# State-space scan into a bilinear feed-forward: the two pairs of a 128-token block share one group of state products and run feed-forward over 512 tokens from block 2 on

## The chip, the cores and the metric

The kernel runs on one core of a Trainium2 chip. Times are device microseconds of one execution; lower is better. Three timed executions of the kernel before are shown, and one profiled execution.

## The reference, cut to what matters

Inputs are x (4 batches, 8 heads, 768 positions, 32 values), a decay a per position, and B and C (16 state values per position). For each batch and head a state of 16 x 32 is carried along the sequence; within a chunk each position also sees the earlier positions through C·B weighted by the decay between them. The result y, put together over the heads to rows of 256, goes through a bilinear feed-forward:

```
cum = cumsum(log a) in the chunk;  L = exp(cum_i - cum_j), i >= j
y   = ((C B^T) * L) x  +  (C state) * exp(cum)
state = exp(sum log a) * state + sum_j exp(cum_last - cum_j) B_j x_j
x2  = y, all heads of a token side by side        (3072 tokens, 256)
out = ((x2 @ w_a) * (x2 @ w_b)) @ w_out           (256 -> 1536 -> 256)
```

The chunk length does not change the mathematics; the kernel uses 128 positions.

## The kernel before, in words

**Tiling.** The sequence is cut into six blocks of 128 positions, and the four batches into two pairs, so there are twelve pairs p = 0 to 11; pair p belongs to block p // 2. A pair is 256 tokens: two batches, 128 positions. Inside a pair the positions are held as 64 partitions times two (r), batch after batch, so that 128 partitions hold both batches. All matrix operands are in 16-bit floats, all sums in 32-bit PSUM.

**Steps of one pair.** `load` (L131) brings B, C and x in six transfers from SP's queue. GpSimd scales B and C by the decay factors and x by a constant (`scale_bc`, `scale_x`, L238 to L269), writing B and C as six 128-column planes; `turn` (L306) transposes the planes with one DMA transpose, also from SP. `scores` (L312) makes C·B for all eight heads in 32 small matmuls into four PSUM banks (SC0 and SC1, two banks each; bank m holds heads 2m and 2m+1). `mask` (L345) multiplies a bank by the causal mask and puts it into SBUF as 16-bit (tile T1): VectorE does it, or, with by_pool, ScalarE copies the bank to SBUF and GpSimd multiplies. `outputs` (L418) then writes y into the first 128 columns of the same four banks: 8 matmuls of the carried state with C (L425), 32 of T1 with x (`pv_u`, L363), and 16 for the new state sums (`ds_mm`, L380) into columns 256 to 319 of two of the banks. ScalarE moves y to SBUF (tile X2T, three instructions, L441); VectorE adds the new state sums to the carried state (`state_sums`, L468, tile U), and GpSimd prepares from it the state operand of the next block (`state_spread`, L484, and the decayed copy gU, L491).

**Feed-forward.** A unit (L529) is two of the twelve 128-wide slices of d_ff for the 256 tokens of a pair: four matmuls of 256 columns with w_a into a PSUM bank, four with w_b into another (L504), a ScalarE copy of the first to SBUF (L518, tile asb), and a VectorE product of the second with it (L525, tile hk). Six units make a pair. `out_half` (L557) multiplies the hidden values of 128 tokens with w_out in twelve matmuls of 256 columns (L538), ScalarE scales the result to SBUF (L553) and SP's queue stores it.

**PSUM.** Four of the eight banks are SC0 and SC1. The other four are a pool (psf) which every unit takes two of and every out_half one, in turn; so a bank is written again four takings later, and only once ScalarE or VectorE has read it.

**Order.** The kernel is scheduled by hand: each engine runs its instructions in the order in which the program issues them. The start (pairs 0 to 2, weights, factors) is written out. From pair 3 on one loop (L704) does, for each pair p: scores of p; GpSimd's preparation and the transpose of p+1, the state operand of p-1, the loads of p+2; then the masks of p between the units of pair p-1 and the first output half of p-2; outputs and state sums of p; the second output half of p-2; the last two units of p-1. The last pair's feed-forward stands after the loop.

The SBUF pool `mid` (three buffers per tile name) holds T1, the scaled x and B, the transposed planes and GpSimd's temporary; `ffh` (four buffers) holds hk, asb and the output rows.

Of the kernel before, what the change touches and what calls it, by code (L numbers as in the profile page):

```python
# [22 lines left out]
def kernel(  # L23
# [60 lines left out]
    X2T = big.tile([128, NP, 2, 2, Q], f16, name="X2T")  # L84
# [17 lines left out]
    mid = ctx.enter_context(tc.tile_pool(name="mid", bufs=3))  # L102
    ffh = ctx.enter_context(tc.tile_pool(name="ffh", bufs=4))
    ps4 = ctx.enter_context(tc.tile_pool(name="ps4", bufs=1, space=PSUM))
# [313 lines left out]
    def outputs(p):  # L418
        s = st[p]
        SCt = (SC0, SC1)  # L420
        for m in range(4):
            for bt in range(2):
                rows = slice(32 * m, 32 * m + 32)
                half = 64 * ((m + bt) % 2)
                nc.tensor.matmul(  # L425
                    SCt[bt][half : half + 64, m // 2, 0:Q],
                    s["Sbd"][rows, bt],
                    s["CT"][rows, bt],
                    start=True,
                    stop=False,  # L430
                    skip_group_check=True,
                    tile_position=(32 * m, half),
                )
        py = {(bt, u): SCt[bt][:, u, 0:Q] for bt in range(2) for u in range(2)}
        for u in range(2):
            pv_u(p, u, py, False)
        if p // NBP < NBLK - 1:
            ds_mm(p, 256, [SC0[:, 1], SC1[:, 1]])
        whole, low, high = slice(0, 128), slice(0, 64), slice(64, 128)
        for bt, to, fr in ((0, whole, whole), (1, low, high), (1, high, low)):  # L440
            nc.scalar.activation(  # L441
                out=X2T[to, p, bt].rearrange("p u (i r) -> p u r i", r=2),
                in_=SCt[bt][fr, :, 0:Q].rearrange("p u (r i) -> p u r i", r=2),
                func=AF.Copy,
                scale=YS / XS,
            )
# [114 lines left out]


# [141 lines left out]
    for p in range(3, NP):  # L704
        scores(p)
        ri = p >= P0
        if p + 1 < NP:
            scale_bc(p + 1, 1, nc.gpsimd)
            scale_bc(p + 1, 0, nc.gpsimd)
            turn(p + 1)  # L710
        if (p - 1) // NBP < NBLK - 1:
            state_spread(p - 1)
        if p + 1 < NP:
            scale_x(p + 1, nc.gpsimd)
        if p + 2 < NP:
            load(p + 2)
        if p == 3:
            mask(product(p, 0))
            h()
            for m in range(1, 4):  # L720
                mask(product(p, m))
            out_half(1, 0)
            out_half(1, 1)
            go((2, 2))
        else:
            h = unit(p - 1, 0)
            mask(product(p, 0), ri=ri)
            h()
            mask(product(p, 1), ri=ri)
            mask(product(p, 2), ri=ri)  # L730
            h = unit(p - 1, 1)
            h()
            mask(product(p, 3), ri=ri)
            go((p - 1, 2))
            out_half(p - 2, 0)
            go((p - 1, 3))
        pull(p)
        outputs(p) if ri else pv(p)
        if p // NBP < NBLK - 1:
            state_sums(p)  # L740
        if p == 3:
            go((2, 3))
        else:
            out_half(p - 2, 1)
        if p % 2 == 0 and p // 2 + 1 < NBLK:
            fb(p // 2 + 1)
        go((p - 1, 4), (p - 1, 5))

    go((NP - 1, 0), (NP - 1, 1))
    out_half(NP - 2, 0)  # L750
    go((NP - 1, 2), (NP - 1, 3))
    out_half(NP - 2, 1)
# [51 lines left out]
```

## Time and profile before

| | |
|---|---|
| three timed executions | 127.15, 129.27, 129.0 us; median 129.0 |
| profiled execution, its own time | 127.25 us |
| its span in the profile | 125.5 us |
| TensorE (PE) busy | 119.9 us, 96% |
| weight loads (PEld) busy | 101.3 us, 81% |
| VectorE (DVE) busy | 88.8 us, 71% |
| ScalarE (ACT) busy | 72.5 us, 58% |
| GpSimd (POOL) busy | 56.6 us, 45% |
| granted TensorE clock in the profiled execution | 1.0 |

Times of the profile count from the start of the span. Matmuls are pipelined: the start of one to the start of the next is what one costs, and the duration printed for one (273 ns for 256 columns) is longer than that. A timeline line merges instructions of one kind that follow each other: start, length, engine, line, shapes, count, and in brackets how long the engine had been idle and what ended it. "SPq" is SP's queue issuing a DMA.

### The profile page before, as it was taken

The numbers are of one execution on the slowest core, as the hardware profiler recorded it, in microseconds if no ns is written. First come the engines' busy times: TensorE is split into PE (matmuls) and PEld (weight loads), VectorE is DVE, ScalarE is ACT, GpSimd is POOL, SyncE is SP. The second block draws the span as 40 slices with busy tenths as digits, with TensorE's granted clock in tenths as the row PEclk, the third lists the DMA queues.
The fourth block names the chain that finished last, engine by engine and source line by source line (L and its number), as shares of the span: only waits on it lengthen the run. The fifth ranks groups of instructions, "written<-read, shape, count | busy, mean of one in ns | idle before, by whom it ended". The sixth has DMA issues, their size and how long they took to land.

```text
span 125.5 us, 4786 instructions
## 1 busy us (share of the span) xinstructions
PE 119.9 (96%) x1964; PEld 101.3 (81%) x1964; DVE 88.8 (71%) x165; ACT 72.5 (58%) x144; POOL 56.6 (45%) x100
## 2 busy tenths in 40 slices
PE   6979999999999999999999999999999999999990
PEld 2436789978898988888898898889889889899980
DVE  1588978894958958948959949959849739644440
ACT  0466666866365575575575475485485575674430
POOL 7999974957850933806508307508218000000000
PEclk9999999999999999999999999999999999999999
DMA  3999999974644666547646764454646210110112
GB/s 65 167 167 232 157 213 159 184 145 80 167 89 67 165 115 125 141 71 185 81 74 169 87 107 128 88 108 126 114 82 168 66 42 5 42 42 5 44 45 78
DMA packets 45493, 13.79 MB, mean 110 GB/s; under 512 B 40496, under 2 KB 45264, under 8 KB 45472
## 3 DMA queue, kind: packets, MB, share of 16 engines
q1 hardware_dynamic: 41520, 10.06, 38.4%
q0 software_dynamic: 1952, 3.08, 14.6%
q10 hardware_dynamic: 2000, 0.36, 1.6%
q8 instruction: 15, 0.25, 0.9%
q14 instruction: 6, 0.05, 0.1%
HBM read 11.13 MB, written 3.15 MB: 114 GB/s over the span
## 4 chain that ended last, share of the span: by engine, by line
PE 84%; DMA 6%; POOL 4%; DVE 2%; ACT 1%; issue 1%; ACTq 0%; POOLq 0%
PE aps L504 25%; PE bps L504 24%; PE ops L538 23%; DMA Wb<-in_moe_w_b_dram 6%; PE SC L320 3%; PE SC L363 3%; DVE t L354 2%; PE SC L380 1%; PE SC L425 1%; PE fps L221 1%; POOL cn L126 1%; PE ops L759 1%; POOL bn L126 1%; ACT bt L297 1%; POOL causal L181 1%
## 5 line engine op out<-in xcount | busy, mean ns | idle before, releaser
L525 DVE TENSOR_TENSOR hk<-bps,asb 128x512 f16<-128x512 f32 x72 | 49.1, 686 | 17.8 <-ACT asb L518 17.4
L518 ACT COPY asb<-aps 128x512 f32<-128x512 f32 x72 | 42.0, 586 | 17.4 <-PE aps L504 16.3
L504 PE MATMUL aps<-X2T,Wa 128*128 128x256 f16 x288 | 43.3, 273 | 0.0
L504 PE MATMUL bps<-X2T,Wb 128*128 128x256 f16 x288 | 42.9, 273 | 0.2 <-DMA Wb<-in_moe_w_b_dram 0.2
L538 PE MATMUL ops<-Wo,hk 128*128 128x256 f16 x276 | 33.9, 273 | 0.0
L504 PEld LDWEIGHTS <-Wb 128*128 128x128 f16 x288 | 29.6, 103 | 2.2 <-DMA Wb<-in_moe_w_b_dram 0.4
L504 PEld LDWEIGHTS <-Wa 128*128 128x128 f16 x288 | 28.5, 103 | 3.0 <-DMA Wa<-in_moe_w_a_dram 0.3
L538 PEld LDWEIGHTS <-hk 128*128 128x128 f16 x276 | 26.0, 98 | 3.6 <-DVE hk L525 0.2
L354 DVE TENSOR_TENSOR t<-SC,causal_ri 128x512 f16<-128x512 f32 x32 | 21.1, 680 | 0.0
L251 POOL TENSOR_TENSOR planes<-cn,fC 128x256 f16<-128x256 f32 x8 | 5.0, 621 | 33.7 <-DMA cn<-in_C_dram 23.1
L553 ACT ACTIVATE osb<-ops 128x256 f32<-128x256 f32 x23 | 8.8, 383 | 16.4 <-PE ops L538 16.2
L245 POOL TENSOR_SCALAR x<-xn 128x512 f16<-128x512 f32 x9 | 13.4, 1490 | 1.0 <-DMA xn<-in_x_dram 0.3
L441 ACT ACTIVATE X2T<-SC 64x256 f16<-64x256 f32 (+1 forms) x24 | 10.9, 456 | 4.9 <-PE SC L380 3.8
L468 DVE SCALAR_TENSOR_TENSOR U<-SC,G,gU 128x64 f32<-128x64 f32 x16 | 4.3, 282 | 7.0 <-ACT X2T L441 6.3
L354 DVE TENSOR_TENSOR t<-SC,causal 128x512 f16<-128x512 f32 x13 | 8.3, 682 | 0.9 <-PE SC L320 0.9
L259 POOL TENSOR_TENSOR bm<-bn,fB 128x256 f16<-128x256 f32 x11 | 7.0, 640 | 1.5 <-DMA bn<-in_B_dram 1.5
L193 PE MATMUL SC<-warm 128*128 128x512 f16 (+1 forms) x15 | 4.9, 474 | 1.2 <-DVE warm L162 1.2
L193 PEld LDWEIGHTS <-warm 128*128 128x128 f16 x22 | 2.3, 122 | 3.7 <-issue 1.9
L363 PEld LDWEIGHTS <-x 64*32 64x32 f16 x384 | 3.2, 91 | 2.2 <-ACT x L243 1.0
L363 PE MATMUL SC<-t,x 64*32 64x128 f16 x352 | 4.6, 219 | 0.0
L269 POOL COPY planes<-bm 128x128 f16<-128x128 f16 x16 | 4.2, 291 | 0.5
L352 POOL TENSOR_TENSOR t<-tmp,causal 128x512 f16<-128x512 f32 x3 | 3.5, 1156 | 1.3 <-DMA cn<-in_C_dram 1.0
(78 smaller groups left out, 81.0 us busy)
## 6 DMA issues: line engine op xcount, KB each, us to landing
out_dram<-osb SPq DMA_DIRECT2D x23, 128.0 KB, 2.5
xn<-in_x_dram SPq DMA_DIRECT2D x21, 128.0 KB, 3.8
bn<-in_B_dram SPq DMA_DIRECT2D x20, 64.0 KB, 3.0
cn<-in_C_dram SPq DMA_DIRECT2D x18, 64.0 KB, 3.1
Wa<-in_moe_w_a_dram POOLq DMA_DIRECT2D x2, 384.0 KB, 6.1
Wb<-in_moe_w_b_dram POOLq DMA_DIRECT2D x2, 384.0 KB, 7.5
Wo<-in_moe_w_out_dram POOLq DMA_DIRECT2D x2, 384.0 KB, 7.0
cn<-in_C_dram POOLq DMA_DIRECT2D x4, 64.0 KB, 5.2
```

Of the source, the lines that this page charges most:

```text
L193: nc.tensor.matmul(bank[:, 0:cols], warm[:, 0:128], warm[:, 0:cols], start=True, stop=True, skip_group_check=True)
L245: eng.tensor_scalar(xo, xi, XS, None, ALU.mult)
L251: eng.tensor_tensor(out=planes[p % 2][:, 4:6].rearrange("p r (h n) -> p r h n", n=N), in0=pair_in[p][which].rearrange("p h r n -> p r h n" ...
L259: eng.tensor_tensor(out=m_, in0=pair_in[p][which].rearrange("p h r n -> p r h n"), in1=(f[:, blk, :, bp] if factor is None else factor).un ...
L354: nc.vector.tensor_tensor(out=o_, in0=i_, in1=c_, op=ALU.mult)
L363: nc.tensor.matmul(py[bt, u][32 * (g ^ 2 * bt) : 32 * (g ^ 2 * bt) + 32] if p >= P0 else py[bt][32 * g : 32 * g + 32, u * Q : (u + 1) * Q] ...
L441: nc.scalar.activation(out=X2T[to, p, bt].rearrange("p u (i r) -> p u r i", r=2), in_=SCt[bt][fr, :, 0:Q].rearrange("p u (r i) -> p u r i" ...
L504: nc.tensor.matmul(ps[:, kk * 2 * Q : (kk + 1) * 2 * Q], W[k // 6][:, f, k % 6 // 3 * 384 : (k % 6 // 3 + 1) * 384].rearrange("p (c kk) -> ...
L518: (nc.vector.tensor_copy if on_dve else nc.scalar.copy)(asb, a_ps)
L525: nc.vector.tensor_tensor(out=s["hk"][:, 2 * k2 : 2 * k2 + 2, :].rearrange("p k q -> p (k q)"), in0=b_ps, in1=asb, op=ALU.mult)
L538: nc.tensor.matmul(o_ps[:, 0:d_model], hk[:, k, bt * Q : (bt + 1) * Q], Wo[:, k, :], start=(k == 0), stop=(k == NK - 1), skip_group_check= ...
L553: nc.scalar.activation(out=o_sb, in_=o_ps[:, 0:d_model], func=AF.Copy, scale=1.0 / (YS * YS))
```

## The change

From block 2 on (pairs 4 to 11) the two pairs of a block are treated together.

- `outputs` takes a block: the state products of both pairs, then T1 with x of both, then the state sums of both, into different columns of the same banks (y in columns 0 to 127 and 128 to 255, state sums from column 256). ScalarE moves both pairs' y in three instructions of 512 elements a partition into a new tile XB. The state sums of both pairs follow.
- `bunit` is one slice of d_ff for the 512 tokens of a block: two matmuls of 512 columns with w_a, two with w_b, then the same ScalarE copy and VectorE product. Twelve make a block. `bout` is `out_half` on a quarter of a block; its rows are stored in the order in which the columns stand.
- The loop is replaced by an order written out. One mask of pairs 5 to 8 is done by ScalarE and GpSimd. Preparation and transpose run two pairs ahead and loads three pairs ahead, from pair 4's stage on; the transition prepares pairs 5 and 6 both in the stage of pair 4. GpSimd's queue has the mask of pair p behind the scaling of x of pair p+1 in pair 5's stage (behind x of pair 6).
- `mid` has four buffers per tile name.

```diff
-    for p in range(3, NP):
-        scores(p)
        ...
-        pull(p)
-        outputs(p) if ri else pv(p)
        ...
+    def outputs(blk):
+        pairs = range(blk * NBP, (blk + 1) * NBP)
+        cols = [slice(j * Q, (j + 1) * Q) for j in range(NBP)]
+        for j, p in enumerate(pairs):
+            s = st[p]
+            for m in range(4):
+                for bt in range(2):
                    ...
+                    nc.tensor.matmul(
+                        SCt[bt][half : half + 64, m // 2, cols[j]],
+                        s["Sbd"][rows, bt],
+                        s["CT"][rows, bt],
+                        start=(j == 0),
                        ...
+        for j, p in enumerate(pairs):
+            py = {(bt, u): SCt[bt][:, u, cols[j]] for bt in range(2) for u in range(2)}
+            for u in range(2):
+                pv_u(p, u, py, False)
+        if blk < NBLK - 1:
+            for j, p in enumerate(pairs):
+                ds_mm(p, NBP * Q + 2 * D * j, [SC0[:, 1], SC1[:, 1]])
        ...
+    def bunit(blk, k):
+        for W in (Wa, Wb):
+            t_ = psf.tile([128, 512], f32, name="aps" if W is Wa else "bps", tag="ff")
+            for f in range(2):
+                nc.tensor.matmul(
+                    t_,
                    ...
+                    XB[:, blk - P0 // NBP, f].rearrange("p t j q -> p (t j q)"),
                    ...
+            ps.append(t_)
+        asb = evac_a(ps[0])
+        return lambda: nc.vector.tensor_tensor(out=s["hk"][:, k], in0=ps[1], in1=asb, op=ALU.mult)
+
+    def stage(p, by_pool, spread=()):
+        scores(p)
+        if by_pool:
+            mask(product(p, 3), by_pool=True, ri=True)
+        if p % NBP == 0 and p // NBP + 1 < NBLK:
+            fb(p // NBP + 1)
+        prep(p + 2, spread)
+        prep_x(p + 2)
+        loads(p + 3, (0, 1, 2))
+
+    scores(3)
+    loads(5, (1, 0))
+    prep(4, (2,))
+    prep_x(4)
+    loads(5, (2,))
    ...
+    scores(4)
+    loads(6, (1, 0))
+    fb(3)
+    prep(5, (3,))
+    prep_x(5)
+    loads(6, (2,))
+    prep(6)
+    prep_x(6)
+    loads(7, (0, 1, 2))
+    masked(4, (0, 1))
+    out_half(2, 0)
+    masked(4, (2, 3), *pu(3, 0, 1, 2, 3))
+    stage(5, True)
+    masked(5, (0, 1))
+    out_half(2, 1)
+    masked(5, (2,), *pu(3, 4, 5))
+    group(2)
+    out_half(3, 0)
+    out_half(3, 1)
+
+    stage(6, True, (4, 5))
+    masked(6, (0, 1))
+    masked(6, (2,), *bu(2, 0, 1, 2, 3, 4))
+    stage(7, True)
+    masked(7, (0, 1, 2), *bu(2, 5, 6, 7, 8, 9, 10, 11))
+    group(3)
+    bout(2, 0)
+    bout(2, 1)
+
+    stage(8, True, (6, 7))
+    masked(8, (0, 1))
+    masked(8, (2,), *bu(3, 0, 1, 2, 3, 4, 5))
+    for blk in range(4, NBLK):
+        pB = blk * NBP + 1
+        stage(pB, False)
+        masked(pB, (0, 1))
+        bout(blk - 2, 2)
+        masked(pB, (2, 3), *bu(blk - 1, 6, 7, 8, 9))
+        group(blk)
+        bout(blk - 2, 3)
+        bgo(blk - 1, 10, 11)
+        if blk + 1 < NBLK:
+            stage(pB + 1, False, (pB - 1, pB))
+            masked(pB + 1, (0, 1))
+            bout(blk - 1, 0)
+            masked(pB + 1, (2,))
+            bout(blk - 1, 1)
+            masked(pB + 1, (3,), *bu(blk, 0, 1, 2, 3, 4, 5))
```

`masked` issues, for each index, the matmuls and the ScalarE copy of a unit, then a mask, then the unit's VectorE product; `prep` is scaling of C and B, the transpose and the state operands; `group` is `outputs` of a block and its state sums. After the loop come the rest of block 4's outputs and block 5's twelve `bunit` and four `bout`.

## The prediction

> **What bounds the kernel now.** I read the page's busy shares and the chain that ended last, then TensorE's timeline over one pair, VectorE's over the same stretch, and SP's and GpSimd's where the new order starts.
>
> ```profile
> PE 119.9 (96%) x1964; PEld 101.3 (81%) x1964; DVE 88.8 (71%) x165; ACT 72.5 (58%) x144; POOL 56.6 (45%) x100
> PE 84%; DMA 6%; POOL 4%; DVE 2%; ACT 1%; issue 1%; ACTq 0%; POOLq 0%
> ```
>
> TensorE is the bound: 84% of the chain is its own work, and from 13 us to 122.4 us the chain holds little else. An edit saves what it takes off TensorE's issue time, and loses every gap that it opens there.
>
> ```profile
> 43.70 0.60 PE L504 MATMUL bps<-X2T,Wb 128*128 128x256 f16 x4
> 44.23 0.26 PE L425 MATMUL SC<-turned,spair 32*64 32x128 f16 x8
> 44.42 0.42 PE L363 MATMUL SC<-t,x 64*32 64x128 f16 x32
> 44.67 0.32 PE L380 MATMUL SC<-x,bm 64*32 64x64 f16 x16
> 44.93 1.49 PE L538 MATMUL ops<-Wo,hk 128*128 128x256 f16 x12
> 47.56 0.60 PE L504 MATMUL bps<-X2T,Wb 128*128 128x256 f16 x4
> 48.09 0.43 PE L320 MATMUL SC<-turned 32*64 32x128 f16 x32
> 48.45 0.62 PE L504 MATMUL aps<-X2T,Wa 128*128 128x256 f16 x4
> ```
>
> Starts count. Four 256-column matmuls take 0.437 us (43.26 to 43.70), so one is 0.1092. The scores of pairs 4 and 5 start at 38.95 and 48.09: a period of 9.14 us, of which 72 feed-forward matmuls are 7.86. The rest is the scores (47.56 + 0.437 = 48.00 to 48.45, and 0.02 in the next matmul: 0.47) and the outputs (44.14 to 44.93, and 0.01: 0.80), each with 0.09 of switching in. 7.86 + 0.47 + 0.80 = 9.13: no gap is left in the period.
>
> ```profile
> 40.59 0.69 DVE L525 TENSOR_TENSOR hk<-bps,asb 128x512 f16<-128x512 f32 x1
> 41.19 1.28 DVE L354 TENSOR_TENSOR t<-SC,causal_ri 128x512 f16<-128x512 f32 x2
> 42.39 0.68 DVE L525 TENSOR_TENSOR hk<-bps,asb 128x512 f16<-128x512 f32 x1
> 45.74 0.28 DVE L468 SCALAR_TENSOR_TENSOR U<-SC,G,gU 128x64 f32<-128x64 f32 x1 [0.53 <-ACT X2T L441]
> 46.61 0.28 DVE L468 SCALAR_TENSOR_TENSOR U<-SC,G,gU 128x64 f32<-128x64 f32 x1 [0.59 <-ACT X2T L441]
> ```
>
> Back to back, VectorE starts a mask or a product every 0.598 us (40.59, 41.19, 42.39), and a result is there 0.686 after its start. Ten a pair are 5.98 of 9.14, but masks come in a burst after scores; today they are spread over two units, a third, and an output half that needs no VectorE.
>
> ```profile
> 31.10 1.03 SPq L555 DMA_DIRECT2D out_dram<-osb  x2
> 33.99 1.33 SPq L308 DMA_TRANSPOSE turned<-planes  x1
> 35.43 1.29 SPq L126 DMA_DIRECT2D bn<-in_B_dram  x2
> 36.83 1.27 SPq L126 DMA_DIRECT2D cn<-in_C_dram  x2
> 38.15 2.46 SPq L126 DMA_DIRECT2D xn<-in_x_dram  x2
> 26.64 1.16 POOL L352 TENSOR_TENSOR t<-tmp,causal 128x512 f16<-128x512 f32 x1 [1.03 <-DMA cn<-in_C_dram]
> 43.50 1.49 POOL L245 TENSOR_SCALAR x<-xn 128x512 f16<-128x512 f32 x1
> ```
>
> SP is a queue of its own: 0.65 us a load, 1.3 a transpose, 1.0 for two stores; six loads of a pair in a row take 4.5 to 5.3, against 3.9 at 0.65, so a stretch of 0.6 to 1.4 falls somewhere among them. Between 30 and 100 us a load of x lands 3.0 to 4.0 after its issue, median 3.5.
>
> **What the Trainium skill says.** "TensorE: Matmul & The Clock Gate", section "Wait — 56ns, not 53.3ns?": a warm matmul costs its columns at 2.4 GHz and 2.5 ns more, 215.7 ns for 512. The trace agrees: 109.2 for 256, and two warm-up matmuls of 512 columns start 0.216 apart (7.55 and 7.77 us). The same page, "Architectural detail: the array is 16× 32×32, not 1× 128×128", has ScalarE and VectorE as strict queues; in the trace they keep the program's order. "PSUM — Partial Sum Buffer", section "PSUM bank collisions raise a hardware error": two engines may not read one bank together; here U waits 0.53 and 0.59 for ScalarE's reads. "GPSIMD Engine Reference", "4.1 Engine selection": GpSimd has no way to PSUM; the mask on it is two steps here, 0.585 of ScalarE and 1.156 of GpSimd.
>
> **What it saves on TensorE.**
> - *512 columns.* Pairs 4 to 11 have 384 matmuls with w_a and w_b; they become 192: 192 x (2 x 0.1092 - 0.2158) = 0.50 us. The twelve output matmuls of each 128 tokens stay as they are.
> - *Shared outputs.* Twice 0.80 becomes 0.80 plus the second pair's bare work: one batch of 8 state products 0.056, four batches of T1 with x 0.224 (their starts are 0.056 apart inside 44.42 to 44.67), 16 state sums at 0.0083, 0.133. 1.21 against 1.60: 0.39 a block, 1.56 for four.
>
> Together 2.06. ScalarE's moves go from six of 0.457 to three of about 0.59 (128x512: L416 0.597) a block, about 1 us less of an engine with slack: nothing on the path. They and the four U behind them (1.8 + 0.8, starting 0.2 after the sums) must end before the next scores; two bout of 1.31 cover 2.62, so I put 0.04 each for blocks 2 and 3, counted as nothing. Stores have the same size and count, off the path. The new fourth buffers cost nothing.
>
> **What it opens: VectorE late after scores.** In the stages of pairs 6 and 8 three masks stand in VectorE's queue ahead of the first product, and TensorE goes straight into units, with no output half between. From the end of scores: TensorE wants the bank for w_b of the third unit after five halves of 0.432, at 2.16. That bank is free after the first product: first mask at 0.23 (ScalarE and VectorE start 0.2 after the last matmul's issue: 43.70 to 43.90), three masks 1.79, product 0.69, 0.06 to TensorE: 2.77. Wait 0.61, twice: 1.22. In pair 7's stage seven units follow with three masks between; the ScalarE copy for the GpSimd mask holds back unit 5's copy, so its product starts 1.41 after scores, the next at 2.60 and 3.80 (a mask before each). Banks of units 8 and 9 come free at 3.35 and 4.55, wanted at 3.02 and 4.21: 0.33 each, 0.66. The same count for the other places (the fourth unit of pair 4's stage 0.14, units 9 of blocks 3 and 4 0.17 each, one output 0.07) gives 0.55. Sum 2.43. Bounds: 1.2 if only the first kind is real, 3.0 if each DVE step is 0.04 longer.
>
> **What it opens: the mask on GpSimd of pair 5.** It stands in GpSimd's queue behind the scaling of x of pair 6, which waits for that load; behind the mask stand the preparations of pair 7, and the outputs of block 2 wait for it on TensorE. SP from 32.13 (the stores of 31.10): B and C of pair 5, 2.6; transpose 4, 1.3; x of 5, 1.3 and 0.4 of stretch; two stores 1.0; B and C of 6, 2.6; transpose 5, 1.3, to 42.6; x of 6 with another 0.4, the second at about 43.7. It lands 3.5 later, 47.2; scaling 1.49, mask 1.16, 0.1 to TensorE: 49.95. TensorE gets there: scores 38.95 + 0.38; output half 1.31; four units 3.49 + 0.14; scores 0.47; output half 1.31; two units 1.75; switch, states and the T1 products up to bank 3's, 0.68: 48.48. Wait 1.5. With no stretch 0.7; with 0.9 twice and a landing of 4.0, 2.9 (then transpose 5, landing 2.9 after 42.6 or later, is also late for scores at 44.4, inside this sum). I take 1.5. Pairs 7 and 8: their masks have 1.5 us or more to spare by the same count, so nothing. Transposes and loads later run a pair further ahead, at no cost.
>
> **Sum.** -2.06 + 2.43 + 1.5 = +1.9 us. Against the profiled execution, 127.25 becomes 129.1. The runs lie at two levels, 127.15 and 127.25, 129.0 and 129.27, which nothing in the trace explains; their mean is 128.2 and the median shown 129.0. From the mean: **130.0 us**.
>
> **The rivals** (same base of 128.2).
> - *Transfers bunch* (0.22). Loads of three pairs crowd the stages of pairs 3 and 4; landings of 5 us also delay the mask of pair 7 and the state operands of block 4. For: the stretches above, and DMA engines already 55% busy at 30 to 40 us. Against: landings in the loop never exceed 4.0 for x. Another 2.2: 132.3, slower.
> - *VectorE keeps up* (0.10), the other side. Place: the third unit after scores. It decides from where the first product frees its bank within 2.16 us of the scores' end, as when TensorE is released later than the queue count says. Price 2.43: -2.06 + 1.5 = -0.6, 127.6, slightly faster. For: DVE is only 71% busy. Against: the 0.598 step is steady in the trace.
> - *x of pair 6 in time* (0.15). Deciding point: landed by 45.7. -2.06 + 2.43 = +0.4: 128.6.
> - *Sharing saves nothing* (0.08): each pair's products still pay the switch because array tiles change all the same. -0.50 + 3.9 = +3.4: 131.6. Against: batches of one shape follow 0.056 apart today.
>
> **How the numbers follow.** The forecast has 0.45. Its own span is 129.0 to 131.1 by the bounds of its two waits. 2% is 2.6 us, about what a measurement of this kernel tells from no change. Faster by more than that exceeds all the savings unless both waits fail and the level falls well: 0.05. Slower by more: the bunching case nearly whole, most of the fourth rival, and the upper part of the forecast: 0.37. The rest, 0.58. The range runs from the VectorE rival at the lower level of runs, 127.3, to the bunching case a little past its middle, 133.0.
>
> **What would show it.** Right: w_a and w_b matmuls 0.216 apart; one outputs group of about 1.2 us a block; TensorE idle about 0.6 us in the third unit after scores of pairs 6 and 8, ended by VectorE; a gap of 1 to 2 us in the first group's T1 products, ended by GpSimd, whose scaling of x waited for a DMA. Wrong: no such gaps, or waits for transposes before scores, or groups of 1.5 us.

## The result: 142.5 us against 128.7, and the profile after

The changed kernel takes 142.48 us (median of four executions, 141.18 to 143.40). The kernel before took 128.68 beside it (127.15 to 129.27). The ratio is 1.108, with a 95% interval of 1.090 to 1.126: slower, far outside the range of the forecast. Here and below, medians are of all executions, and ratios leave out those more than 1.5% above the fastest of their kernel. The profiled execution took 143.4 us, with a span of 141.6; the span before was 125.5, so 16.1 us have to be found.

The page of the changed kernel, busy shares and the chain that ended last (by engine, then by line):

```profile
PE 120.3 (85%) x1772; PEld 82.3 (58%) x1772; DVE 86.2 (61%) x161; ACT 70.9 (50%) x136; POOL 61.3 (43%) x104
PE 51%; DMA 24%; POOL 6%; SPq 6%; issue 3%; ACT 2%; DVE 0%; POOLq 0%; ACTq 0%
PE aps L578 14%; PE bps L578 13%; PE ops L605 10%; DMA out_dram<-osb 10%; DMA cn<-in_C_dram 6%; DMA Wb<-in_moe_w_b_dram 6%; SPq L128 5%; PE bps L511 3%; DMA xn<-in_x_dram 3%; PE ops L545 3%; PE aps L511 2%; PE SC L322 1%; PE SC L365 1%; POOL x L247 1%; PE fps L223 1%
```

TensorE's share of the chain fell from 84% to 51%, and DMA's rose from 6% to 24%; 10% of the span, 14 us, are stores of output rows. No store was in the chain that the forecast read.

**The tail.** The timeline from 117.8 us on, SP's queue, ScalarE, VectorE and ScalarE's queue:

```profile
117.83 14.35 SPq L618 DMA_DIRECT2D out_dram<-osb  x6
...
127.84 0.38 ACT L617 ACTIVATE osb<-ops 128x256 f32<-128x256 f32 x1 [0.93 <-PE ops L605]
129.33 0.29 DVE L615 TENSOR_SCALAR osb<-ops 128x128 f32<-128x128 f32 x1 [5.86 <-DMA out_dram<-osb]
132.03 0.28 ACT L617 ACTIVATE osb<-ops 128x128 f32<-128x128 f32 x1 [3.81 <-DMA out_dram<-osb]
132.34 1.10 ACTq L618 DMA_DIRECT2D out_dram<-osb  x1
```

TensorE's last matmul starts at 128.92, but the second half of the last rows' columns is read from PSUM only at 132.03, because its output buffer still waits for an older store, and the end comes at 141.6. Before, 3.4 us lay between the last matmul (122.14) and the end; now 12.7 do. The same stretch by windows (length, busy time of PE, PEld, DVE, ACT and POOL with counts, PEclk, DMA share, GB/s), first of the kernel after, then of the kernel before:

```profile
130.00:141.60 11.60, 0.00 (x0) 0.00 (x0) 0.00 (x0) 0.28 (x1) 0.00 (x0) 0.60 0.12 40
```

```profile
122.30:125.50 3.20, 0.06 (x2) 0.00 (x0) 0.00 (x0) 0.28 (x1) 0.00 (x0) 1.00 0.26 82
```

For 11.6 us almost nothing runs but stores, and they keep 0.12 of 16 DMA engines busy: about two engines. The packets of the trace say the same. From its first row to its last, a store of 128 rows takes 3.26 us (118.97 to 122.23), where one took 0.47 before (119.19 to 119.67), while a packet of one row takes 46 to 47 ns at the median in both. Estimated from these figures, 64 packets one after the other are 2.9 us and 8 are 0.37: the rows go over two engines instead of sixteen. Behind the rows of one store stand two packets of 4 bytes; before, there were 16. The rows are the same. What differs is how the destination is walked: "(i r) d -> r i d" makes it 2 x 64 x 256, with the 2 outermost.

**The middle.** TensorE's timeline in the stages of pairs 6 and 7, with the second shared group:

```profile
58.32 0.43 PE L322 MATMUL SC<-turned 32*64 32x128 f16 x32
...
60.43 0.59 PE L578 MATMUL aps<-XB,Wa 128*128 128x512 f16 x2
60.89 0.59 PE L578 MATMUL bps<-XB,Wb 128*128 128x512 f16 x2
...
67.46 0.59 PE L578 MATMUL bps<-XB,Wb 128*128 128x512 f16 x2
68.06 0.59 PE L578 MATMUL aps<-XB,Wa 128*128 128x512 f16 x2
...
69.87 0.32 PE L430 MATMUL SC<-turned,spair 32*64 32x128 f16 x16
70.12 0.73 PE L365 MATMUL SC<-t,x 64*32 64x128 f16 x64
70.74 0.46 PE L382 MATMUL SC<-x,bm 64*32 64x64 f16 x32
71.13 2.79 PE L605 MATMUL ops<-Wo,hkb 128*128 128x256 f16 x24
```

Two matmuls of 512 columns take 0.431 us, as forecast. In the third unit after the scores of pair 6, where 0.61 us of waiting for VectorE was forecast, the bank for w_b is reached 0.46 after that for w_a: 0.03 of waiting.

**The start of the new order.** TensorE from 38 to 60 us, and GpSimd beside it:

```profile
41.34 0.43 PE L322 MATMUL SC<-turned 32*64 32x128 f16 x32 [1.79 <-DMA turned<-planes]
...
47.18 0.43 PE L322 MATMUL SC<-turned 32*64 32x128 f16 x32 [0.50 <-DMA turned<-planes]
...
53.62 0.32 PE L365 MATMUL SC<-t,x 64*32 64x128 f16 x12 [2.04 <-POOL t L354]
54.13 4.26 PE L545 MATMUL ops<-Wo,hk 128*128 128x256 f16 x24
```

```profile
50.85 1.49 POOL L247 TENSOR_SCALAR x<-xn 128x512 f16<-128x512 f32 x1 [3.13 <-DMA xn<-in_x_dram]
52.41 1.15 POOL L354 TENSOR_TENSOR t<-tmp,causal_ri 128x512 f16<-128x512 f32 x1
```

The mask of pair 5 stands behind x of pair 6, as forecast, and TensorE waits 2.04 us for it. Two more things were not in the sum: TensorE waits for the transposes of pairs 4 and 5 (1.79 and 0.50), and after the stop its clock is lower: from the start of 24 output matmuls to the next scores 4.19 us pass (54.13 to 58.32), where 24 starts at full clock are 2.62.

**Where the 16.1 us are.** Tail 9.3 (12.7 less 3.4); transposes 2.3; mask 2.0; clock 1.6; one stop at 88.3 us 1.4; small waits for VectorE and ScalarE about 0.8; a start that was 0.5 later before the new order begins. That is 17.9, less about 1.9 saved: 16.0.

### The profile page after: what moved, and what is told of

The parts are those of the page before. It is cut to its first block, busy times and chain, and to the rows that moved or that the text cites. A ratio compares the mean times of both kernels' runs of the same rounds, so it can differ in the third digit from the quotient of the medians.

```text
span 141.6 us, 4384 instructions
## 1 busy us (share of the span) xinstructions
PE 120.3 (85%) x1772; PEld 82.3 (58%) x1772; DVE 86.2 (61%) x161; ACT 70.9 (50%) x136; POOL 61.3 (43%) x104
## 3 DMA queue, kind: packets, MB, share of 16 engines
HBM read 11.13 MB, written 3.15 MB: 101 GB/s over the span
## 4 chain that ended last, share of the span: by engine, by line
PE 51%; DMA 24%; POOL 6%; SPq 6%; issue 3%; ACT 2%; DVE 0%; POOLq 0%; ACTq 0%
PE aps L578 14%; PE bps L578 13%; PE ops L605 10%; DMA out_dram<-osb 10%; DMA cn<-in_C_dram 6%; DMA Wb<-in_moe_w_b_dram 6%; SPq L128 5%; PE bps L511 3%; DMA xn<-in_x_dram 3%; PE ops L545 3%; PE aps L511 2%; PE SC L322 1%; PE SC L365 1%; POOL x L247 1%; PE fps L223 1%
## 5 line engine op out<-in xcount | busy, mean ns | idle before, releaser
L590 DVE TENSOR_TENSOR hkb<-bps,asb 128x512 f16<-128x512 f32 x48 | 32.3, 689 | 13.6 <-ACT asb L525 12.9
L578 PE MATMUL aps<-XB,Wa 128*128 128x512 f16 x96 | 28.6, 380 | 1.2 <-DVE U L475 1.2
L578 PE MATMUL bps<-XB,Wb 128*128 128x512 f16 x96 | 28.5, 379 | 0.0
L605 PE MATMUL ops<-Wo,hkb 128*128 128x256 f16 (+1 forms) x204 | 22.5, 267 | 0.0
L605 PEld LDWEIGHTS <-hkb 128*128 128x128 f16 x204 | 18.5, 98 | 3.0
L356 DVE TENSOR_TENSOR t<-SC,causal_ri 128x512 f16<-128x512 f32 x28 | 17.9, 683 | 3.2 <-PE SC L322 3.2
L532 DVE TENSOR_TENSOR hk<-bps,asb 128x512 f16<-128x512 f32 x24 | 16.1, 684 | 4.1 <-ACT asb L525 3.8
L578 PEld LDWEIGHTS <-Wa 128*128 128x128 f16 x96 | 9.6, 103 | 10.6 <-issue 2.1
L511 PE MATMUL aps<-X2T,Wa 128*128 128x256 f16 x96 | 14.3, 274 | 0.7 <-DMA Wa<-in_moe_w_a_dram 0.7
L511 PE MATMUL bps<-X2T,Wb 128*128 128x256 f16 x96 | 14.1, 273 | 0.3 <-DMA Wb<-in_moe_w_b_dram 0.3
L545 PE MATMUL ops<-Wo,hk 128*128 128x256 f16 x96 | 13.0, 295 | 0.0
L545 PEld LDWEIGHTS <-hk 128*128 128x128 f16 x96 | 9.6, 106 | 2.1
```

What stands on the lines that cost most here:

```text
L356: nc.vector.tensor_tensor(out=o_, in0=i_, in1=c_, op=ALU.mult)
L511: nc.tensor.matmul(ps[:, kk * 2 * Q : (kk + 1) * 2 * Q], W[k // 6][:, f, k % 6 // 3 * 384 : (k % 6 // 3 + 1) * 384].rearrange("p (c kk) -> ...
L532: nc.vector.tensor_tensor(out=s["hk"][:, 2 * k2 : 2 * k2 + 2, :].rearrange("p k q -> p (k q)"), in0=b_ps, in1=asb, op=ALU.mult)
L545: nc.tensor.matmul(o_ps[:, 0:d_model], hk[:, k, bt * Q : (bt + 1) * Q], Wo[:, k, :], start=(k == 0), stop=(k == NK - 1), skip_group_check= ...
L578: nc.tensor.matmul(t_, W[k // 6][:, f, k % 6 // 3 * 384 : (k % 6 // 3 + 1) * 384].rearrange("p (c kk) -> p kk c", kk=3)[:, k % 3], XB[:, b ...
L590: return lambda: nc.vector.tensor_tensor(out=s["hk"][:, k], in0=ps[1], in1=asb, op=ALU.mult)
```

## The experiments

The kernel before was timed again beside each group of runs, on the same chip; its medians were 128.17, 127.47, 127.20, 127.52 and 127.03 us.

### Rows stored whole

The product of the feed-forward writes its result in the order of tokens, so that a store is 128 whole rows again.

```diff
-        return lambda: nc.vector.tensor_tensor(out=s["hk"][:, k], in0=ps[1], in1=asb, op=ALU.mult)
+        return lambda: nc.vector.tensor_tensor(
+            out=s["hk"][:, k].rearrange("p (c i r) -> p c r i", c=2 * NBP, r=2),
+            in0=ps[1].rearrange("p (c r i) -> p c r i", c=2 * NBP, r=2),
...
-        rows = out[(2 * j + bt) * S + blk * Q :][0:Q].rearrange("(i r) d -> r i d", r=2)
+        rows = out[(2 * j + bt) * S + blk * Q :][0:Q]
```

> The changed kernel with one part undone: each quarter of a block is stored as 128 consecutive rows, as before the change (VectorE's product writes hk in token order, so the store needs no row order of its own); instruction counts are the same. Theory S (the new store, whose destination has a slowest dimension of 2, runs on two of the sixteen DMA engines, 3.2 us for 128 rows where it took 0.5): the 12.5 us between the last matmul and the end go back to about 3, and the 1.6 us stop of TensorE at 88 us goes with them; what stays is the start-up loss of the new order (waits for the transposes of pairs 4 and 5 and for GpSimd's mask of pair 5, 4.3 us, and 1.6 us of a lower clock after them). 130 to 132 us, 11 us below the changed kernel. Rival O (the four buffers of output rows are the limit, whatever the store's shape): 140 to 142. Rival F (512-column feed-forward or the shared groups cost the time): 140 to 142.

Measured: 131.9 us (129.51 to 132.99), ratio 1.018 (1.006 to 1.030). Of the 10.8% by which the change slowed the kernel, 1.8% is left; by the medians 10.6 us are gone. The stretch behind the last matmul, by windows:

```profile
127.90:131.20 3.30, 0.18 (x4) 0.01 (x1) 0.00 (x0) 0.28 (x1) 0.00 (x0) 0.86 0.26 79
```

The tail is 3.3 us again, with twice the DMA share. What is left, TensorE's timeline:

```profile
53.85 0.29 PE L365 MATMUL SC<-t,x 64*32 64x128 f16 x12 [2.33 <-POOL t L354]
...
54.32 4.46 PE L545 MATMUL ops<-Wo,hk 128*128 128x256 f16 x24
```

No transpose is late in this profile, which the forecast of this run did not expect. TensorE's granted clock was 0.5 from 10.83 to 17.65 us, and it came to the scores of pair 4 only at 41.83; so this profile doesn't show that the late transposes are cured.

### The kernel before, its rows stored in the changed kernel's way

```diff
-                out=X2T[to, p, bt].rearrange("p u (i r) -> p u r i", r=2),
-                in_=SCt[bt][fr, :, 0:Q].rearrange("p u (r i) -> p u r i", r=2),
+                out=X2T[to, p, bt],
+                in_=SCt[bt][fr, :, 0:Q],
...
+        if p >= P0:
+            rows = rows.rearrange("(i r) d -> r i d", r=2)
```

> The kernel before with the new store alone: from pair 4 on ScalarE moves y without reordering and the store puts the rows into token order in its destination pattern. Theory S: the last five stores now queue on two engines, 3.2 us for a full one and 1.7 for a half-width one, so the end comes 4 to 5 us later: 131.5 to 134; more if the loads that share these engines get late. Rivals O and F: 127 to 129.5, as before.

Measured: 139.59 us (138.12 to 142.49), ratio 1.083 (1.072 to 1.094). More than either range. The tail is 8.5 us (132.2 to 140.75), 5.1 more than before, and TensorE waits before scores:

```profile
78.23 0.43 PE L320 MATMUL SC<-turned 32*64 32x128 f16 x32 [1.05 <-DMA turned<-planes]
...
88.53 0.43 PE L320 MATMUL SC<-turned 32*64 32x128 f16 x32 [1.09 <-DMA turned<-planes]
...
101.00 0.65 PE L320 MATMUL SC<-turned 32*64 32x128 f16 x32 [3.27 <-DMA turned<-planes]
```

So the store alone, put into a kernel whose loads and transposes had no trouble, costs 8.3%, 10.6 us. The profile is of the slowest execution, 15.3 us above the span before: 5.1 are the tail, 5.4 are transposes that come late while stores are on their way, and about 2.9 are a lower clock behind the last of these waits (0.5 from 100.17 to 107.00). Some 1.6 were lost before the first changed store was issued: the scores of pair 6 start at 58.84 in place of 57.23, after a clock of 0.5 between 11.43 and 14.84. In the changed kernel no transpose is late once such stores run; why it is spared was not tried.

### Sixteen buffers for output rows

```diff
+    osbp = ctx.enter_context(tc.tile_pool(name="osbp", bufs=16))
...
-            o_sb = ffh.tile([128, d_model], f32, name="osb", tag="osb")
+            o_sb = osbp.tile([128, d_model], f32, name="osb", tag="osb")
```

> The changed kernel with sixteen buffers of output rows instead of four and nothing else. Theory S: VectorE and ScalarE no longer wait for a store at the end (5.9 and 3.8 us today), but the stores still queue on two engines and end when they did: 140.5 to 143. Rival O: the 9 us come back, 131 to 134.

Measured: 142.23 us (141.31 to 143.18), ratio 1.112 (1.103 to 1.121): no gain. The timeline of the tail:

```profile
128.12 0.29 DVE L616 TENSOR_SCALAR osb<-ops 128x128 f32<-128x128 f32 x1 [5.03 <-PE ops L606]
128.79 0.28 ACT L618 ACTIVATE osb<-ops 128x128 f32<-128x128 f32 x1 [0.96 <-PE ops L606]
```

Nobody waits for a buffer now, yet the end stays at 141.5: the stores themselves are the limit, not the buffers that they hold. Here too a transpose is late while stores run: TensorE waits 2.94 us for one, up to 88.65.

### Two stores of 64 rows

```diff
-            (nc.sync, nc.scalar)[part].dma_start(rows[:, :, cs], o_sb[:, 0:w])
+            for r in range(2):
+                (nc.sync, nc.scalar)[part].dma_start(rows[r, :, cs], o_sb[64 * r : 64 * r + 64, 0:w])
```

> The changed kernel with one edit: each store of 128 rows becomes two of 64 rows, one for even and one for odd tokens, so that a destination walks over 64 rows at its outermost step and not over 2. Bytes, row order in SBUF and the product with asb stay. If the outermost step of the destination sets how many DMA engines work: stores take 0.3 to 0.6 us each, the end comes 3 to 4 us after the last matmul, and the time is 131 to 133, as with whole rows. If it is the stride of 2 rows in memory or the number of rows: the stores stay at 3 us and the time at 142. SP has one more issue for each store, 0.55 us, which may add up to 1 us.

Measured: 132.73 us (129.9 to 135.64), ratio 1.024 (1.007 to 1.041). Same bytes, same stride of two rows in memory, same SBUF order; the outermost step of the destination went from 2 to 64, there are twice as many stores, and 10 us are gone. The page has, in us to landing at the median:

```profile
out_dram<-osb SPq DMA_DIRECT2D x30, 64.0 KB, 2.0
```

Each of these stores has 16 packets of 4 bytes behind its rows again. The tail is 5.2 us, not 3 to 4, since SP issues ten stores where it issued five. This settles the store: its outermost dimension, not its stride and not the product.

### Whole rows, transposes first, the mask of pair 5 on VectorE

With the rows mended, the rest was attacked at once: transposes 4 and 5 ahead of the loads of pairs 5 and 6 in SP's queue, and all four masks of pair 5 on VectorE.

```diff
     scores(3)
-    loads(5, (1, 0))
     prep(4, (2,))
     prep_x(4)
-    loads(5, (2,))
+    loads(5, (1, 0, 2))
...
-    stage(5, True)
+    stage(5, False)
```

> The plain store, and the start of the new order mended: the transposes of pairs 4 and 5 stand ahead of the loads of pairs 5 and 6 on SP's queue again, and the fourth mask of pair 5 is VectorE's instead of GpSimd's. Theory S with the start-up losses as read from the trace (turn 4 1.8, turn 5 0.5, mask 2.0, clock 1.6): these 5.9 us go too, and what is left are the savings on TensorE (2.1) less some small gaps: 125.5 to 127, 1 to 2 us below the kernel before. If instead the new order costs TensorE in the later stages too: 127.5 to 130.

Measured: 135.95 us (134.75 to 141.49), against 128.17 beside it. The expectation was wrong, by 8 to 9 us. TensorE's timeline:

```profile
45.71 0.43 PE L322 MATMUL SC<-turned 32*64 32x128 f16 x32 [1.02 <-DMA turned<-planes]
49.99 0.31 PE L430 MATMUL SC<-turned,spair 32*64 32x128 f16 x15 [0.52 <-DVE t L356]
54.85 0.43 PE L322 MATMUL SC<-turned 32*64 32x128 f16 x32 [0.92 <-DMA turned<-planes]
63.00 0.43 PE L322 MATMUL SC<-turned 32*64 32x128 f16 x32 [3.15 <-DMA turned<-planes]
```

The wait at pair 4 is gone, and waits of 1.02, 0.92 and 3.15 stand at pairs 5, 6 and 7. Loads that went behind a transpose came late, and so did the transposes that need them.

### The mask of pair 5 ahead of x of pair 6

From here on rows are stored whole. In GpSimd's queue the mask goes first.

```diff
     prep(6)
-    prep_x(6)
     loads(7, (0, 1, 2))
...
             mask(product(p, 3), by_pool=True, ri=True)
+        if p == 5:
+            prep_x(6)
```

> Rows stored whole, as in the first experiment, and in GpSimd's queue the mask of pair 5 ahead of the scaling of x of pair 6. Queue theory (GpSimd's mask waits for x of pair 6 and TensorE's clock falls after that stop): the stop of 2.0 to 2.3 us in the first group's T1 products and the 1.6 to 1.8 us of lower clock behind it are gone; 131.9 becomes 127.5 to 128.5, with a wait of 1 to 2 us for the transpose of pair 4 or 5 left. Rival (the mask is late by itself, or TensorE waits there for something else): the stop stays above 1 us and the time above 130.

Measured: 130.7 us (128.91 to 134.4), ratio 1.018 (1.005 to 1.031). The stop for the mask of pair 5 is gone from the trace, so that cause was right; the gain is not there. The profile is of the slowest execution (134.4; the others took 128.91 to 130.79). TensorE's waits from 30 us on (total, times, longest):

```profile
PE SC L322 <- DMA turned<-planes: 4.7, 3, 2.1
PE SC L365 <- POOL t L354: 1.7, 1, 1.7
```

Three transposes are late (pairs 4, 5 and 7), and now the mask of pair 7, behind the preparation of pair 9, which waits for its load.

### The same, stores of pairs 0 to 3 from ScalarE's queue

```diff
-        out_store(p, bt, o_ps)
+        out_store(p, bt, o_ps, q=nc.scalar)
```

> As the run before it, and the eight stores of pairs 0 to 3 are issued by ScalarE's queue in place of SP's. If the late transposes of pairs 4 and 5 come from a full SP queue: each store is about 0.55 us less on SP, the transposes go out 1 us or more earlier, and the time is 125.5 to 127.0, below the kernel before. If the transposes wait for the landing of loads, or ScalarE's own copies come late behind its DMA issues (about 0.55 to 1.1 us each): no gain, 127.5 to 129.5, and TensorE waits for ScalarE in the output halves of pairs 0 to 3.

Measured: 131.05 us (130.15 to 133.92), ratio 1.023 (1.011 to 1.035). The transposes of pairs 4 and 5 are in time; ScalarE is not. Its timeline at 54 us:

```profile
53.98 0.38 ACT L560 ACTIVATE osb<-ops 128x256 f32<-128x256 f32 x1 [0.43 <-PE ops L545]
56.50 0.34 ACTq L562 DMA_DIRECT2D out_dram<-osb  x1
56.96 0.58 ACT L353 COPY tmp<-SC 128x512 f32<-128x512 f32 x1 [2.60 <-DMA turned<-planes]
```

The issue costs ScalarE only 0.34, but it is held for 2.1 us. In the program each of these DMAs waits until the one eight before it, with the same semaphore, has landed; for this store that is the transpose of pair 7, issued at 53.45 and landed at 56.43. ScalarE's copies stand behind it, and TensorE waited 1.94 for one. The rival held in its mechanism; the time is above its range of 127.5 to 129.5.

### The feed-forward banks taken strictly in turn

The four banks get four names, used in rotation; otherwise as the run with the mask ahead.

```diff
-            t_ = psf.tile([128, 512], f32, name="aps" if W is Wa else "bps", tag="ff")
+            t_ = psf.tile([128, 512], f32, name="aps" if W is Wa else "bps", tag=in_turn())
```

> As the run with the mask ahead, but the four feed-forward banks are taken strictly in turn, so that each is written again four takings later. Theory (the predicted waits for VectorE are small because banks are handed out in the order in which they come free): with banks in turn TensorE waits about 0.6 us in the third unit after the scores of pairs 6 and 8, ended by VectorE, and the time is 1.2 to 2.4 us above that run. Rival (VectorE simply is earlier than the prediction's count): no such waits, the same time within 0.5 us.

Measured: 131.38 us (130.49 to 132.28), ratio 1.028 (1.017 to 1.039). Against the other run's 1.018 the times say nothing. The waits do:

```profile
PE SC L327 <- DMA turned<-planes: 2.2, 1, 2.2
PE bps L583 <- DVE hkb L595: 1.1, 4, 0.4
```

Four waits for VectorE's product, of 0.36 in the third unit after the scores of pairs 6 and 8 and of 0.15 and 0.18 in pair 7's stage. The changed kernel's list of waits has none for a product. Banks handed out as they come free are why most of the forecast waits are missing; but in turn they are 1.1 us in all, not 2.4. The one late transpose here is that of pair 4: with the same order of loads as the run before, the waits at pairs 5 and 7 and for the mask of pair 7 are absent. Such waits differ from one execution to the next.

### Loads ahead of the transpose before them

```diff
+        loads(p + 3, (0, 1))
         prep(p + 2, spread)
         prep_x(p + 2)
-        loads(p + 3, (0, 1, 2))
+        loads(p + 3, (2,))
```

and likewise the loads of pair 7 ahead of the transpose of pair 6.

> As the run with the mask ahead (130.7), and from pair 7 on the loads of B and C of a pair stand in SP's queue ahead of the transpose of the pair before, no longer behind it. Theory (a pair's loads are issued only after the transpose before them, which itself waits for loads: a ring of landing, scaling, transpose and issue of about 9 us that never catches up): the waits before the scores of pairs 6 and 7 and the late mask of pair 7 behind a late load go (1.0 + 1.7 in that profile), the waits for the transposes of pairs 4 and 5 stay (2.1 + 1.5); 128.0 to 129.5. Rival (DMA engines or the DMAs in flight are the limit, not the order): nothing gained, 130 to 131.5.

Measured: 129.2 us (20 executions, 127.81 to 131.65), ratio 1.010 (1.007 to 1.014). TensorE's wait for transposes:

```profile
PE SC L322 <- DMA turned<-planes: 2.7, 2, 2.1
```

Against the run with the mask ahead, the waits for the transpose of pair 5 (1.50) and for the mask of pair 7 (1.73) are gone, that for the transpose of pair 7 fell from 1.06 to 0.60, and that at pair 4 stays at 2.10. That the ring of load, scaling, transpose and next load was part of the loss isn't shown by this: the banks in turn, with the old order of loads, lacked most of these waits too, and the times of the two orders overlap (1.010 and 1.018).

### Early loads, early transposes; and units ahead of scores

Three more orders of SP's queue and TensorE, all on top of the loads ahead of the transposes. The first loads B and C of pair 5 ahead of the two stores of pair 0, and puts the transposes of pairs 4 and 5 earlier:

```diff
     load(4)
+    tiles(5)
+    for bt in range(2):
+        load1(nc.sync, 5, 1, bt)
+    for bt in range(2):
+        load1(nc.sync, 5, 0, bt)
...
     prep(4, (2,))
     prep_x(4)
+    st00()
+    st01()
     loads(5, (2,))
```

> As the run before it, and at the start of the new order: B and C of pair 5 are loaded ahead of the two stores of pair 0, the transpose of pair 4 goes ahead of those stores, and the transpose of pair 5 goes ahead of the loads of pair 6. Theory (late transposes of pairs 4 and 5 come from SP's queue alone): no wait above 0.5 us before the scores of pairs 4 to 7; 125.5 to 127.0, below the kernel before. Rival (each step taken forward delays the next, as when the transposes alone went first: 135.95): waits of 1 us or more turn up at pair 6 or 7, and the time is 128 to 131.

The second gives TensorE other work before the scores that wait:

```diff
-    go((2, 3), (2, 4), (2, 5))
+    go((2, 3), (2, 4), (2, 5), (3, 0), (3, 1))
...
-    masked(6, (2,), *bu(2, 0, 1, 2, 3, 4))
+    masked(6, (2,), *bu(2, 0, 1, 2, 3, 4, 5))
```

> As the run with the loads ahead of the transposes (129.2), and on TensorE alone: two units of pair 3 (1.75 us) go from behind the scores of pair 4 to ahead of them, and one unit of block 2 (0.86 us) from behind the scores of pair 7 to ahead of them. Theory (what is left of the loss is TensorE standing before these scores for their transposes, 2.1 and 0.6 us, with work at hand that could run meanwhile): the wait at pair 4 falls to about 0.35, that at pair 7 to 0; 126.7 to 127.5, level with or just below the kernel before. Rival (the time is lost again later, at the next transpose or at the first group for a mask that now starts later): 128.5 or more, with a wait of 1 us or more at pair 5 or in the first group.

The third has both edits.

> As the run with the early loads and the early transposes (129.47), with the same three units moved ahead of the scores. Theory: the waits of 1.55 and 1.33 us in that profile fall to 0 and about 0.5; 126 to 127, below the kernel before (127.2 to 128.2). Rival: 128.5 or more, as in the run beside it.

Measured: 129.47, 129.55 (19 executions, 126.9 to 133.09) and 129.52 us; ratios 1.012 (1.001 to 1.023), 1.005 (0.9995 to 1.0095) and 1.014 (1.007 to 1.020). Only five of the second's 19 executions enter its ratio, and the median of all 19 lies 1.6% above that of the kernel before, so it isn't shown to be level. None beats it. TensorE's waits for transposes, in this order:

```profile
PE SC L322 <- DMA turned<-planes: 2.9, 2, 1.6
```

```profile
PE SC L322 <- DMA turned<-planes: 2.7, 3, 1.8
```

```profile
PE SC L322 <- DMA turned<-planes: 2.0, 1, 2.0
```

They stood at pairs 4 and 7, at 4, 5 and 7, and at 6 (with 0.5 for VectorE at pair 5). Two to three microseconds of waiting move about and stay.

### Sharing from block 3 on

Block 2 keeps the outputs and the feed-forward of the kernel before; the written-out order starts two pairs later.

```diff
+    for p in (4, 5):
+        scores(p)
+        prep(p + 1, (p - 1,))
...
+        outputs1(p)
...
+    scores(6)
+    fb(4)
+    prep(7, (5,))
```

> Rows stored whole and loads ahead of transposes as before, but block 2 keeps the kernel before's per-pair outputs and feed-forward; sharing and 512 tokens start with block 3. TensorE saves three quarters of 2.06 us, 1.5. Theory (the start of sharing pulls the loads of one more pair into the stretch from 30 to 60 us, where the DMA engines are busiest): the same pull now falls between 48 and 80 us; if that stretch has room, no wait above 0.5 us before scores, and 126 to 127, below the kernel before (127.2 to 128.2). Rival (the shared groups themselves cost what they save): as with block 2, 128.5 to 130.

Measured: 130.28 us (128.53 to 131.89), against 127.03 beside it. TensorE's waits:

```profile
PE SC L323 <- DMA turned<-planes: 2.4, 2, 2.0
```

The wait of 2.0 us is there again, at 64.55 us, before the scores of pair 7, the second of the new order. Starting two pairs later did not take it away: the expectation of 126 to 127 was wrong.

### Without x of pairs 5, 6 and 7

The run with both edits, with six transfers of 128 KB left out: x of pair 4 is used for pairs 5 to 7.

```diff
+                if w == 2 and p in (5, 6, 7):
+                    continue
                 for bt in range(2):
                     load1(nc.sync, p, w, bt)
```

> As the run with early loads, early transposes and units ahead of scores (129.5), but the loads of x of pairs 5, 6 and 7 are left out, and x of pair 4 is used in their place: six transfers of 128 KB fewer between 38 and 60 us. Theory (loads and transposes of that stretch are short of DMA time): the wait of 1.96 us for the transpose of pair 6 goes, 127 to 127.8. Rival (the transposes wait for GpSimd or for their place in the order, not for the amount of loads): the wait stays above 1 us, 129 or more.

Measured: 126.8 us (eight executions, 126.6 to 128.51), ratio 0.9991 (0.9973 to 1.0010). TensorE's waits:

```profile
PE SC L322 <- DVE t L356: 0.5, 1, 0.5
```

No transpose is late. The windows from 35 to 60 us, of the kernel before, of the run with both edits, and of this one:

```profile
35.00:60.00 25.00, 25.00 (x456) 21.99 (x454) 19.23 (x35) 15.36 (x31) 11.58 (x21) 1.00 0.56 120
```

```profile
35.00:60.00 25.00, 22.40 (x412) 17.53 (x410) 17.70 (x34) 13.47 (x25) 14.75 (x22) 1.00 0.74 128
```

```profile
35.00:60.00 25.00, 24.45 (x447) 18.07 (x446) 19.55 (x36) 15.38 (x29) 18.57 (x29) 1.00 0.60 126
```

TensorE, busy all the time before, stood still for 2.6 us with both edits, and gets 2.05 of them back. That these six loads decide is shown. By which way is not, since they left the DMA engines, SP's queue and the eight semaphores in rotation alike, and GpSimd waited less for x (3.9 us between 35 and 62 us with both edits, 0.7 without these loads).

## Why the prediction was wrong, point by point

**The step that failed: "Stores have the same size and count, off the path."** Size and count are the same; the walk is not. The diff shows `rearrange("(i r) d -> r i d", r=2)` on the destination, and the forecast took from it only the order of rows. "DMA: Bandwidth & Descriptors", section "Why a DMA increments its semaphore by 16 and not by 1", has the rule: a transfer runs on the largest number of engines up to 16 that divides the slowest dimension, other than 1, of both access patterns. With 64 or 128 outermost that is 16, with 2 it is 2. The traces agree: 0.12 of 16 engines in the tail, and 3.26 us against 0.47 for a store. At the end TensorE has 128 new rows every 1.31 us, and each store of them takes 3.3. The step's price was 9.3 us in the span, and 10 to 11 by the medians of the two runs that mended the store.

**"Transposes and loads later run a pair further ahead, at no cost"** failed too, and waits for transposes before scores were the prediction's own sign of being wrong. Scores start at these times (us), read from TensorE's timeline:

| pair | 4 | 5 | 6 | 7 | 8 | 9 | 11 |
|---|---|---|---|---|---|---|---|
| before | 38.95 | 48.09 | 57.23 | 66.36 | 75.50 | 84.64 | 102.76 |
| loads ahead of transposes | 41.37 | 46.74 | 54.21 | 59.87 | 70.71 | 76.56 | 94.49 |

Feed-forward of a block can start only when both its pairs have their outputs, so TensorE takes scores of pair 7 6.5 us and of pair 11 8.3 us sooner, and its feed-forward backlog is a pair longer at the end. The loads of one more pair are due between 30 and 60 us. The forecast counted the issues of that stretch for one late mask, and had a late transpose of pair 5 only in that sum's upper bound; in the changed kernel 2.29 us of late transposes stood beside it, and 2.0 to 2.9 stayed in each order that loaded everything and had the mask ahead but left the stores on SP (4.7 in the first of them).

**The mask of pair 5, 1.5.** Right in mechanism: x of pair 6 landed about 50.8, not 47.2, and the wait was 2.04 (2.33 with whole rows). The mask put ahead of that x took this wait away. Not counted was the lower clock behind it, 1.6.

**VectorE late, 2.43.** Mis-sized. The third unit waits 0.03, the largest wait in the stages of pairs 6 to 8 is 0.17 (67.46 to 68.06 less 0.43), and all of them are about 0.35. The words on the kernel said that a bank is written again four takings later. In the program a bank is handed out when it is released, so the one that ScalarE has read comes first and the one that waits for VectorE's product later. Strictly in turn they cost 1.1 us. The rest of the error is the count itself: 0.61 forecast, 0.36 measured.

**What it saves, 2.06.** Nearly right: 0.431 for two matmuls of 512; a shared group without waits takes 1.25 us (84.88 to 86.13) against the forecast 1.21, so 0.35 a block, 1.4, and 1.9 with the 0.5. The ScalarE moves, "0.04 each", cost 0.10 and 0.09 before and in the scores of pair 8.

**The rivals.** With the store mended in two ways the changed kernel is 1.8% and 2.4% above the kernel before, 2.3 and 3.0 us. The forecast had 1.8 us and "transfers bunch" 4.1; the intervals can't tell them apart. That the forecast comes so near without its error on stores is luck: the 2.43 for VectorE was not there, and a lower clock (in both profiles) and a late transpose (in one), which it had at nothing, stood in its place. The mechanism of "transfers bunch", loads of three pairs in the stages of pairs 3 and 4, fits the late transposes. "VectorE keeps up" was right on VectorE and wrong on the time, since what it left out was larger. "x of pair 6 in time" and "sharing saves nothing" fell.

**What a fed kernel would gain.** Even with six loads left out and no transpose late, the time only equals that of the kernel before (0.9991), although 1.9 us are saved. Of these, 0.5 goes to the wait for VectorE at pair 5 that moving the units made; the rest lies in waits too small for the list, such as 0.27 at 62.8 us and twice 0.21 ahead of the scores after a group. That they add up to the remainder was not shown by a run. The stop at 88.3 us in the changed kernel (1.4), which the list of waits puts down to VectorE's U, is in no other profile at that place and stays open.

## What to carry to other kernels

When a change touches an access pattern of a DMA, read its outermost dimension on both sides before its bytes: with the same rows and the same packets it went from sixteen engines to two. When work is grouped so that one side runs ahead, list by when each load is due in the new order, and which queue and which earlier loads it stands behind; mending one wait in a feed that is short moves it to the next pair. And a saving on the bound engine is worth what is left when the engines that release its buffers are asked the same question bank by bank.

## What the runs showed of the hardware

- Slow stores slow other transfers. In the kernel before, two-engine stores brought 5.4 us of late transposes besides 5.1 at the end. A transpose issued at 92.75 was used at 101.00, 8.2 us later, where without such stores none took more than 4.5 to land. The mean DMA share between 90 and 100 us was 0.86 at only 83 GB/s, against 0.49 at 110. By which way stores held the transposes back was not tried.
- After stops of 2.04 and 2.33 us TensorE's granted clock (the third number from the right) was 0.5 for 3.41 us; after one of 2.10 (loads ahead of transposes) it stayed at 1.0. In all profiles the clock changes only in steps of 3.41 us, which lie differently against the kernel each time. The stop of 2.04 fell into one step, as the first two lines show; that of 2.10 was split over two, 1.09 and 1.00 (last two lines, of the other run):

```profile
50.34:53.75 3.41, 1.38 (x95) 0.94 (x99) 1.21 (x2) 0.58 (x1) 2.64 (x2) 1.00 0.58 96
53.75:57.17 3.42, 3.42 (x59) 2.48 (x47) 1.21 (x5) 2.04 (x4) 2.60 (x5) 0.50 0.47 119
```

```profile
36.95:40.36 3.41, 2.32 (x22) 1.94 (x19) 2.67 (x6) 1.99 (x4) 0.62 (x1) 1.00 1.03 81
40.36:43.77 3.41, 2.40 (x51) 2.15 (x52) 1.97 (x4) 0.47 (x2) 2.70 (x6) 1.00 1.02 202
```

  In eight profiles 1.72 to 2.94 us of idleness within one step were followed by a clock of 0.5; 1.96 us in the run with sharing from block 3 on were not. "TensorE: Matmul & The Clock Gate", section "What's actually happening", lowers the clock after an idle window of about 3.4 us that runs freely. The steps agree with that window, but a window idle for about half of its time was enough here.
- The same throughput can cost more DMA time: between 35 and 60 us 120 GB/s took a share of 0.56 before, and 128 GB/s took 0.74 in the run with both edits. Why was not tried.
